# Sigmoid attention and an MLP mixer on one core: combination sums all on VectorE, the next tokens' loads queued ahead of the transposes, turns allowed anywhere in the opening section

## The chip, the cores and the metric

The kernel runs on one core of a Trainium2 chip. The metric is the device time of one execution in microseconds (us), the median of several runs. The core has five engines that work side by side, each on its own queue of instructions: TensorE (PE in the profile, with its weight loads as PEld), VectorE (DVE), ScalarE (ACT), GpSimd (POOL) and SyncE (SP). An instruction waits, at the head of its engine's queue, until everything that it needs is there, and what stands behind it waits too. DMAs are issued from such queues (here POOL for loads, SP for transposes and stores) and carried out by 16 DMA engines.

## The reference

The inputs are `q`, `k` and `v` with shape (8, 12, 448, 64) (batches, heads, tokens, features), and four weight matrices.

```python
attn = sigmoid(q @ k.T / sqrt(64) - log(448))        # 448 x 448 for each batch and head
x    = (attn @ v), heads side by side                # 8 x 448 x 768
h    = relu(x.T @ w_tok1) @ w_tok2                   # tokens mixed: 448 -> 256 -> 448
u    = x + h.T
h2   = relu(u @ w_ch1) @ w_ch2                       # channels mixed: 768 -> 1536 -> 768
out  = u + h2                                        # float32
```

## The kernel before

**Units.** The work is cut into five units. `A` and `B` are one batch each, taken as two halves of six heads; units 1, 2 and 3 are two batches each, with six pairs of heads. A unit goes through attention (for a pair: `scores` gives `qk`, ScalarE's sigmoid makes `attn` of it at L358, `values` gives `xa`), the token mixing (`tok1`, then `tok2_pair` for each of the seven rows `j` of 64 tokens, which makes `yn` on TensorE and `u = x + yn` on VectorE at L463), and two channel products, `ch1` and `ch2`. Attention and tokens of the unit behind run beside the channel products of the unit ahead; unit 3 is last and its channel products run alone.

**Channel products of units 1 to 3.** They are cut in blocks of 2 by 2 and made with seven products in place of eight. This needs combination sums of blocks. In the first product (`ch1_pieces`, 42 pieces of three matmuls: six column blocks of seven pieces) these are `s1` to `s4`, made from the transposed tokens `uT`; results are collected in PSUM banks, and three snapshots of each block, `c1`, `c6` and `c7` (`save`, L637), are copied out of a bank while it goes on being added to. VectorE then writes `h2T = relu(ps + c)` (`made`, L642) three times a block, and ScalarE a fourth one (L203). The second product (`ch2_pieces`, 25 pieces of six matmuls) has a direct product `d` of two pieces at each end, for the seventh row, and three blocks `n` of seven pieces between them. Each block needs four sums of its own, made by `row_sums` (L541) of `h2T`: `r2`, `r3`, `r4` and one in place, each 128 x 768. Block 0 has them on VectorE; blocks 1 and 2 on GpSimd in units 1 and 2, and on VectorE in unit 3. Each of the pieces of `ch2` ends in an addition to `u` on VectorE (`plus`, L849), and this addition frees the PSUM bank. There are four such banks, `m0` to `m3`: `x` of block `n` is in bank `n % 3`, `z` in bank `(n - 1) % 3`, `y` in `m3`, and the direct products in `m0` (first) and `m1` (second).

**Loads, transposes and stores.** `load_pair` loads `k`, `q` and `v` of a pair from the POOL queue (L219). Buffers of a pair are reused, and a load ahead of its time would stand in the way of other transfers, so GpSimd makes a small copy first, the *gate* (`load_next`, L338), which reads something that must be there before the loads behind it may start: the `qT` of the pair before, or, once the last pair of a unit has been scored (`state["mixing"]`), the last row of `uT` of that unit. GpSimd then brings `k` and `q` into another order (`pk`, `pq`, L279), and from the SP queue DMA transposes make `kT` and `qT` of them (L306). The seven rows of `u` are copied to half precision (`u16`, which takes a slot of the pool of `attn`) and transposed by DMA to `uT` (L478, SP queue). Finished rows of the output are stored from the SP queue too (L704), two stores to a row.

In units A and B, and for the first pair of unit 1, TensorE turns `k` and `q` itself (`turn_by_pe`, `tk` and `tq`, L291).

**What sets the order.** All engines run instructions in the order in which the program was written out. This order comes from a planner (`merge`), which keeps its own clocks for the engines: `did` adds the cost of a step to a clock, and `there` notes when a result is to be had. It takes from several lists: `main` (the pieces of the channel products), `sec` (attention and tokens of the next unit, with due positions in `main`), `side` (the sums, each with a position from which it may be written and one by which it must), `loads` (gates and transposes, as soon as their estimated time has come), `turns` and `quick`. So a change of an engine, a bank or a condition also moves other work. Ahead of `merge`, `first_attention` writes the opening section, unit A's attention, by the same estimates; a candidate there is the step that can start first:

```python
soon = when(quick[0][0]) if quick else None
...
if turns and (soon is None or soon > clock["pe"] + 1.0):
    yield turns[0][0], lambda: turns.pop(0)[1]()
```

## Time and profile before

| | |
|---|---|
| median of the runs | 406.08 us (405.96 to 406.99, 3 runs) |
| the profiled execution | 403.87 us; its span, first to last recorded instruction, 402.1 us |
| granted TensorE clock | 1.0 |
| busy: PE, DVE, ACT, POOL | 361.3, 248.7, 183.4 and 147.5 us |
| idle time of PE within the span | 40.8 us |
| data moved by DMA | 45.43 MB, mean 113 GB/s |

Busy time is the time in which an engine had a recorded instruction running. In the rows of a timeline, the first two numbers are the start and the length in us, then come the engine (`SPq` and `POOLq` are the issue of a DMA from that queue), the line, the operation, and out<-in by the names in the program, without their numbers; the number in brackets is the idle time of the engine ahead of it, and what ended it. Rows of the form "PE x L837 <- DVE u L849: 5.4, 3, 2.1" sum up waits: who waited for whom, for how many us in all, how often, and the longest. A window's row has start, end and length, then for PE, PEld, DVE, ACT, POOL and SP the busy time and in brackets the instructions, then the granted clock, the busy share of the DMA engines and GB/s. Rows that begin with a line number group equal instructions: busy us and mean ns, then idle time ahead of them.

### The profile page before, as it was taken

The numbers are of one execution on the slowest core, as the hardware profiler recorded it, in microseconds if no ns is written. First come the engines' busy times: TensorE is split into PE (matmuls) and PEld (weight loads), VectorE is DVE, ScalarE is ACT, GpSimd is POOL, SyncE is SP. The second block draws the span as 40 slices with busy tenths as digits, with TensorE's granted clock in tenths as the row PEclk, the third lists the DMA queues.
The fourth block names the chain that finished last, engine by engine and source line by source line (L and its number), as shares of the span: only waits on it lengthen the run. The fifth ranks groups of instructions, "written<-read, shape, count | busy, mean of one in ns | idle before, by whom it ended". The sixth has DMA issues, their size and how long they took to land. (4 is left out here: it accounts for less than half of the span.)

```text
span 402.1 us, 8717 instructions
## 1 busy us (share of the span) xinstructions
PE 361.3 (90%) x3600; PEld 186.1 (46%) x3600; DVE 248.7 (62%) x436; ACT 183.4 (46%) x221; POOL 147.5 (37%) x218
## 2 busy tenths in 40 slices
PE   2887999999999997899979999869987999899894
PEld 1444444455544566344435454434443545444552
DVE  1356556566754687787574457736665377887762
ACT  2883465566664210656755553636775341011000
POOL 8754314555555000554578500364561400000000
PEclk9999999999999999999999999999999999999999
DMA  7999997789977234987745956967760237400054
GB/s 101 187 203 206 166 165 117 116 135 152 143 125 117 45 78 100 181 111 99 111 78 98 160 68 133 215 104 102 108 101 2 61 87 134 132 2 0 4 154 119
DMA packets 78279, 45.43 MB, mean 113 GB/s; under 512 B 51872, under 2 KB 75424, under 8 KB 78240
## 3 DMA queue, kind: packets, MB, share of 16 engines
q0 software_dynamic: 24288, 21.93, 37.8%
q1 hardware_dynamic: 53952, 22.95, 27.1%
q8 instruction: 28, 0.46, 0.5%
q14 instruction: 11, 0.09, 0.1%
HBM read 43.84 MB, written 11.01 MB: 136 GB/s over the span
## 5 line engine op out<-in xcount | busy, mean ns | idle before, releaser
L358 ACT ACTIVATE attn<-qk 128x896 f16<-128x896 f32 x126 | 110.0, 915 | 84.0 <-PE qk L351 67.2
L622 PEld LDWEIGHTS <-w 128*128 128x128 f16 x378 | 34.8, 97 | 44.2 <-issue 15.8
L637 DVE COPY c<-x 128x448 f32<-128x448 f32 x54 | 33.5, 620 | 25.4 <-PE x L622 24.6
L351 PE MATMUL qk<-qT,kT 64*64 64x448 f16 x504 | 40.5, 362 | 7.3 <-DMA qT<-pq 5.2
L622 PE MATMUL x<-uT,w 128*128 128x448 f16 x162 | 37.6, 353 | 1.2 <-DVE c L637 0.9
L849 DVE TENSOR_TENSOR u<-u,x 128x384 f32<-128x384 f32 x36 | 19.9, 552 | 17.5 <-PE x L837 17.3
L837 PEld LDWEIGHTS <-h2T 128*128 128x128 f16 x216 | 19.9, 98 | 23.2 <-issue 11.6
L219 POOL DMA_DIRECT2D k<-in_k_dram x36 | 21.4, 602 | 24.6 <-PE tk L291 15.4
L369 PE MATMUL xa<-attn,v 64*64 64x448 f16 x504 | 27.3, 352 | 3.4 <-ACT attn L358 3.4
L351 PEld LDWEIGHTS <-kT 64*64 64x64 f16 x504 | 13.2, 104 | 29.6 <-issue 23.5
L358 ACT ACTIVATE attn_B<-qk_B 128x896 f16<-128x896 f32 x21 | 18.0, 920 | 16.4 <-PE qk_B L351 16.1
L642 DVE CUSTOM_DVE_ANT_0 h2T<-z,c 128x448 f16<-128x448 f32 x36 | 22.5, 624 | 4.2 <-PE z L622 3.4
L622 PE MATMUL z<-s,w 128*128 128x448 f16 x108 | 24.6, 353 | 0.3 <-ACT h2T L203 0.3
L279 POOL COPY pq<-q 128x896 f16<-128x896 f16 x17 | 15.9, 933 | 23.7 <-DMA q<-in_q_dram 23.7
L203 ACT ACTIVATE h2T<-x 128x448 f16<-128x448 f32 x18 | 9.8, 547 | 32.2 <-PE x L622 32.2
L463 DVE TENSOR_TENSOR u<-x_nat,yn 128x384 f32<-128x384 f16 x42 | 21.0, 548 | 4.5 <-PE yn L445 3.6
L219 POOL DMA_DIRECT2D v<-in_v_dram x36 | 22.2, 646 | 1.3 <-DMA k<-in_k_dram 1.3
L358 ACT ACTIVATE attn_A<-qk_A 128x896 f16<-128x896 f32 x21 | 17.7, 928 | 10.2 <-PE qk_A L351 10.2
L219 POOL DMA_DIRECT2D q<-in_q_dram x36 | 21.8, 624 | 1.1 <-PE tq L291 0.9
L837 PE MATMUL x<-w_s,h2T 128*128 128x384 f16 x108 | 20.9, 327 | 0.1
L369 PEld LDWEIGHTS <-v 64*64 64x64 f16 x504 | 13.6, 106 | 15.7 <-issue 8.4
L837 PEld LDWEIGHTS <-r 128*128 128x128 f16 x162 | 14.7, 98 | 12.5 <-issue 3.8
(122 smaller groups left out, 613.0 us busy)
## 6 DMA issues: line engine op xcount, KB each, us to landing
out_dram<-u SPq DMA_DIRECT2D x42, 192.0 KB, 2.9
k<-in_k_dram POOLq DMA_DIRECT2D x36, 112.0 KB, 3.0
q<-in_q_dram POOLq DMA_DIRECT2D x36, 112.0 KB, 4.4
v<-in_v_dram POOLq DMA_DIRECT2D x36, 112.0 KB, 4.5
out_dram<-u SPq DMA_DIRECT2D x28, 96.0 KB, 3.3
w<-in_moe_w_ch_dram POOLq DMA_DIRECT2D x2, 1152.0 KB, 11.8
w<-in_moe_w_ch_dram POOLq DMA_DIRECT2D x1, 2304.0 KB, 18.1
k_A<-in_k_dram POOLq DMA_DIRECT2D x6, 112.0 KB, 4.4
```

Source lines behind the costliest of these rows:

```text
L203: nc.scalar.activation(out=o, in_=x, func=RELU)
L219: nc.gpsimd.dma_start(out=t[64 * side : 64 * side + 64, :, :, :], in_=src[b, h + 2 * i : h + 2 * i + 2].rearrange("h (p j) e -> p h j e", ...
L279: nc.gpsimd.tensor_copy(out=m[:, :, :, :], in_=raws[(g, i, what)].rearrange("p h j e -> p j h e"))
L351: nc.tensor.matmul(out=ps[64 * b : 64 * b + 64, h, 0:S], lhsT=kT[(g, i)][r, j, b, :], rhs=qT[(g, i)][r, :, b, :], start=True, stop=True,)
L358: nc.scalar.activation(out=at[:, :, :], in_=ps[:, :, 0:S], func=SIGMOID, bias=att_bias, scale=att_scale)
L369: nc.tensor.matmul(out=ps[b][64 * h : 64 * h + 64, :], lhsT=vf[r, h, j, :], rhs=attn[(g, i, j)][r, h, :], start=(j == 0), stop=(j == J - 1),)
L463: nc.vector.tensor_tensor(out=u_part(g, j, half), in0=x_of(g, half)[:, j, :], in1=ps[half][:, :], op=ADD)
L622: nc.tensor.matmul(out=ps[:, :], lhsT=W(p, n, cb), rhs=A[p](n), start=(first and n == 0), skip_group_check=True, stop=(n == KD - 1),)
L637: nc.vector.tensor_copy(out=s[:, :], in_=bk[(cb, "x")][:, :])
L642: nc.vector._custom_dve(dve_ops.TENSOR_ADD_SAT, out=h[half][:, cb, :, b, :], in0=ps.rearrange("c (j p) -> c j p", j=J), in1=snap[(cb, n)]. ...
L837: nc.tensor.matmul(out=ps[:, :], lhsT=A(p, n, kb), rhs=W(p, kb), start=(first and kb == 0), skip_group_check=True, stop=(kb == KC - 1),)
L849: nc.vector.tensor_tensor(out=u, in0=u, in1=ps[:, :], op=ADD)
```

## The change

- **Sums.** The block sums of `ch2` are all made on VectorE in units 1 and 2. Block 0's are split: four of the six column blocks (`k` 0 to 4, 512 elements) may be made from piece 31 of the first product on, the rest when that is done. In unit 3 the four sums of that first part go to GpSimd, everything else to VectorE. 
- **Snapshots.** In unit 3, `c1` and `c6` are copied by ScalarE (`BY_ACT`), `c7` as before by VectorE.
- **Banks.** The first direct product uses bank `m3`, the second `m0` (`DIRECT`).
- **Stores.** In unit 3 the second store of each row is issued from ScalarE's queue.
- **Loads.** `load_next` is called two rounds earlier (`LOAD = 1`). The condition of the gate is worked out when it is written, and the `uT` comes into it only from the first row on whose transpose was written (`state["turned"]`), not from the end of scoring on: in the order that results, the gates at the two unit boundaries read `qT` of the pair before.
- **Opening section.** A turn is a candidate at any time.

```diff
@@
     DMAT, DMAU = 1.6, 1.6
     PATIENT = 6
     SLACK = 1.2
+    LOAD = 1
+    BY_ACT = (1, 6)
+    DIRECT = (3, 0)
     FROM = (10, 44)
     LATE, MIX = 8, 46
     TAKE = (5,)
@@
         if at and PAIRS.index(at) >= BY_PE:
             turn_by_dma(*at)
 
-    loads, state = [], {"mixing": None}
+    loads, state = [], {"turned": None}
 
     def load_next(g, i):
 
         at = ahead(g, i, 2)
         if not at or PAIRS.index(at) < BY_PE + 1:
             return
-        t, keys = state["mixing"], [("q", *ahead(g, i, 1))]
-        if t is not None:
-            keys.append(("uT", t, J - 1))
+        def keys():
+            t = state["turned"]
+            return [("q", *ahead(g, i, 1))] + ([("uT", t, J - 1)] if t is not None else [])
 
         def f():
             gate = pa.tile([1, 2], FP16, tag="gate", bufs=2, name=f"gate_{g}_{i}")
-            if t is None:
-                source = qT[ahead(g, i, 1)][0:1, 0, 0, 0:2]
+            last = max(keys(), key=lambda key: there[key])
+            if last[0] == "q":
+                source = qT[last[1:]][0:1, 0, 0, 0:2]
             else:
-                source = uTs[t][0:1, NDB - 1, J - 1, 0, 0:2]
+                source = uTs[last[1]][0:1, NDB - 1, J - 1, 0, 0:2]
             nc.gpsimd.tensor_copy(out=gate[:, :], in_=source)
-            did("pool", 0.2, keys, ["gate"])
+            did("pool", 0.2, keys(), ["gate"])
             load_pair(*at)
 
         loads.append((keys, f))
@@
         copy(engine_of(g), u16[:, :], u_of(g, j)[:, :])
         evac(engine_of(g), D if engine_of(g) == "act" else DH, [("u", g, j)], [("u16", g, j)])
         did("sp", 1.4, [("u16", g, j)], [("uT", g, j)], DMAU)
-        if j == J - 1:
-            state["mixing"] = None
+        state["turned"] = g
         if g not in uTs:
             uTs[g] = pa.tile([128, NDB, J, 2, P], FP16, tag="uT", bufs=1, name=f"uT_{g}")
         nc.sync.dma_start_transpose(
@@
             one(1, engine, s1, a21, a22, ADD, needs),
             one(2, engine, s2, s1, a11, SUB, needs + key(1)),
             one(4, engine, s4, a12, s2, SUB, needs + key(2)),
-            one(3, nc.vector, a21, a11, a21, SUB, needs + key(1)),
+            one(3, engine, a21, a11, a21, SUB, needs + key(1)),
         ]
 
     def ch1_sums(g, j0, j1):
@@
             if p == 1:
                 bk[(cb, "x")] = bank(f"x1_{g}_{cb}", [128, S], at=cb % 3)
                 mm(bk[(cb, "x")], 1, cb, True)
-                save(cb, 1, "dve")
+                save(cb, 1, "act" if g == 3 and 1 in BY_ACT else "dve")
...
@@
         there[("stored", g, j)] = clock["pe"] + 3.5
         did("sp", 1.3, [], [])
         for b in range(2):
-            nc.sync.dma_start(
+            (nc.scalar if g == 3 and b else nc.sync).dma_start(
                 out=out[2 * g + b].rearrange("(p j) d -> p j d", j=J)[:, j, :],
                 in_=us[(g, j)][64 * b : 64 * b + 64, :],
             )
@@
         def blk(half, j):
             return h[half][:, :, j, :, :].rearrange("c k b p -> c k (b p)")
 
-        def sums(n):
-            S2[n] = [
-                pa.tile(
-                    [128, KC, 128],
-                    FP16,
-                    tag=f"s{m}" if n == 1 else f"r{m}",
-                    bufs=1,
-                    name=f"r{m}_{g}_{n}",
-                )
-                for m in (2, 3, 4)
-            ]
+        def sums(n, k0, k1):
+
+            if n not in S2:
+                S2[n] = [
+                    pa.tile(
+                        [128, KC, 128],
+                        FP16,
+                        tag=f"s{m}" if n == 1 else f"r{m}",
+                        bufs=1,
+                        name=f"r{m}_{g}_{n}",
+                    )
+                    for m in (2, 3, 4)
+                ]
+            k = slice(k0, k1)
             return row_sums(
-                nc.gpsimd if n and g < 3 else nc.vector, KC * 128, ("R", g, n), [("h", g)], blk(0, 2 * n), blk(1, 2 * n), blk(0, 2 * n + 1), blk(1, 2 * n + 1), *[s[:, :, :] for s in S2[n]]
+                nc.gpsimd if g == 3 and n == 0 and k1 < KC else nc.vector,
+                (k1 - k0) * 128,
+                ("R", g, n) if k1 == KC else ("r", g, n, k0),
+                [("h", g)],
+                *[
+                    blk(half, j)[:, k, :]
+                    for half, j in ((0, 2 * n), (1, 2 * n), (0, 2 * n + 1), (1, 2 * n + 1))
+                ],
+                *[s[:, k, :] for s in S2[n]],
             )
 
         def A(p, n, kb):
@@
 
         def direct(half, part):
             j = 2 * NB
-            pe(0.49, [("h", g)] + ([f"m{half}"] if part == 0 else []), ["pe"])
+            pe(0.49, [("h", g)] + ([f"m{DIRECT[half]}"] if part == 0 else []), ["pe"])
             if part == 0:
-                bk[("d", half)] = bank(f"d2_{g}_{half}", [128, DH], at=half)
+                bk[("d", half)] = bank(f"d2_{g}_{half}", [128, DH], at=DIRECT[half])
             ps = bk[("d", half)]
             for cb in range(part * KC, part * KC + KC):
                 if cb % KC == KC // 2:
...
@@
                     )
             else:
                 keys = [("raw", *at, "k"), ("raw", *at, "q")]
-                loads.append((keys, lambda: turn_by_dma(*at)))
-        if j == 3:
+                loads.append((lambda: keys, lambda: turn_by_dma(*at)))
+        if j == LOAD:
             load_next(g, i)
 
     def turned_back(g, i):
@@
 
     def value_stay(g, i):
         values(g, i)
-        if i == NPAIR[g] - 1 and g not in SINGLE:
-            state["mixing"] = g
         turned_back(g, i)
 
     def attention_stays(pairs):
@@
             soon = when(quick[0][0]) if quick else None
             if quick:
                 yield quick[0][0], lambda: quick.pop(0)[1]()
-            if turns and (soon is None or soon > clock["pe"] + 1.0):
+            if turns:
                 yield turns[0][0], lambda: turns.pop(0)[1]()
             if w:
                 yield w[0][0], lambda: w.pop(0)[1]()
@@
...
             c2, b1 = base[g] + 42, base[g] + B1
-            for n, first in enumerate((c2, c2, b1)):
+            for n, k0, k1, first, span in (
+                (0, 0, 4, base[g] + 31, 11),
+                (0, 4, KC, c2, 4),
+                (1, 0, KC, c2, 7),
+                (2, 0, KC, b1, 7),
+            ):
+                name = ("R", g, n) if k1 == KC else ("r", g, n, k0)
                 for m in range(4):
-                    done = {0: [], 1: [("R1", g, n)], 2: [("R2", g, n)], 3: [("R1", g, n)]}[m]
-                    side.append((first, first + 4 if n == 0 else first + 7, [("h", g)] + done, block_sum(n, m)))
+                    keys = [("h", g)] + [[], ["1"], ["2"], ["1"]][m]
+                    keys = keys[:1] + [(name[0] + x, *name[1:]) for x in keys[1:]]
+                    side.append((first, first + span, keys, block_sum(n, k0, k1, m)))
 
         def w_sum(m):
             def f():
```

`memo` is the dictionary of the unit's pieces, which the sums now use directly. Further places only pass the new bank numbers and call the keys of `loads` as functions.

What the planner makes of it, at three places. On VectorE, where the first product of unit 2 ends and the second begins (`h2T` the result of the first, `r2` to `r4` the sums, a second `h2T` the sum in place, `d2` the first direct product, `x2` the first block), before:

```order
L642 ISA h2T_2_1_4089<-z1_2_5_4568,c6_2_5_4562 128x7x64
L541 TENSOR_TENSOR r2_2_0_4677<-h2T_2_0_4088,h2T_2_1_4089 128x768
L541 TENSOR_TENSOR r3_2_0_4678<-r2_2_0_4677,h2T_2_0_4088 128x768
L541 TENSOR_TENSOR h2T_2_0_4088<-h2T_2_0_4088 128x6x128
L541 TENSOR_TENSOR r4_2_0_4679<-h2T_2_1_4089,r3_2_0_4678 128x768
L849 TENSOR_TENSOR u_2_6_3972<-u_2_6_3972,d2_2_0_4670 128x384
L541 TENSOR_TENSOR h2T_2_0_4088<-h2T_2_0_4088 128x6x128
L849 TENSOR_TENSOR u_2_0_3828<-u_2_0_3828,x2_2_0_4750 128x384
```

and now:

```order
L645 ISA h2T_2_1_4055<-z1_2_5_4649,c6_2_5_4618 128x7x64
L544 TENSOR_TENSOR r2_2_0_4542<-h2T_2_0_4054,h2T_2_1_4055 128x256
L544 TENSOR_TENSOR r3_2_0_4543<-r2_2_0_4542,h2T_2_0_4054 128x256
L544 TENSOR_TENSOR r4_2_0_4544<-h2T_2_1_4055,r3_2_0_4543 128x256
L544 TENSOR_TENSOR h2T_2_0_4054<-h2T_2_0_4054 128x2x128
L544 TENSOR_TENSOR r2_2_1_4706<-h2T_2_0_4054,h2T_2_1_4055 128x768
L544 TENSOR_TENSOR r3_2_1_4707<-r2_2_1_4706,h2T_2_0_4054 128x768
L544 TENSOR_TENSOR r4_2_1_4708<-h2T_2_1_4055,r3_2_1_4707 128x768
L544 TENSOR_TENSOR h2T_2_0_4054<-h2T_2_0_4054 128x6x128
L863 TENSOR_TENSOR u_2_6_3960<-u_2_6_3960,d2_2_0_4695 128x384
L863 TENSOR_TENSOR u_2_0_3790<-u_2_0_3790,x2_2_0_4758 128x384
```

Two thirds of block 0's sums have moved further ahead, block 1's four sums have come from GpSimd, and the addition of `d2` stands behind all of them.

On the SP queue, where unit 1 ends and unit 2's rows are transposed (`uT_2` those rows, `u_1` the rows of unit 1 that are stored, two stores to a line here, `kT_3_2` and `qT_3_2` the transposes of the third pair of unit 3), before:

```order
L478 DMA_TRANSPOSE uT_2_3833<-u16_2_4_3935 128x6x128
L478 DMA_TRANSPOSE uT_2_3833<-u16_2_5_3954 128x6x128
L704 DMA out_0_dram<-u_1_3_2568 64x768 x2
L478 DMA_TRANSPOSE uT_2_3833<-u16_2_6_3975 128x6x128
L704 DMA out_0_dram<-u_1_4_2587 64x768 x2
L704 DMA out_0_dram<-u_1_5_2679 64x768 x2
L704 DMA out_0_dram<-u_1_6_2711 64x768 x2
L306 DMA_TRANSPOSE kT_3_2_4158<-pk_3_2_4156 128x7x128
L306 DMA_TRANSPOSE qT_3_2_4162<-pq_3_2_4160 128x7x128
```

and now:

```order
L481 DMA_TRANSPOSE uT_2_3795<-u16_2_5_3940 128x6x128
L481 DMA_TRANSPOSE uT_2_3795<-u16_2_6_3963 128x6x128
L707 DMA out_0_dram<-u_1_2_2505 64x768 x2
L707 DMA out_0_dram<-u_1_3_2578 64x768 x2
L707 DMA out_0_dram<-u_1_4_2597 64x768 x2
L707 DMA out_0_dram<-u_1_5_2689 64x768 x2
L707 DMA out_0_dram<-u_1_6_2721 64x768 x2
L309 DMA_TRANSPOSE kT_3_2_4112<-pk_3_2_4110 128x7x128
L309 DMA_TRANSPOSE qT_3_2_4116<-pq_3_2_4114 128x7x128
```

The last transposes of `uT_2` have moved ahead of the stores of rows 2 and 3, and the transposes of the pair stand behind five stored rows.

On VectorE at the end of unit 3's first product (`c1`, `c6`, `c7` the snapshots), before:

```order
L637 COPY c1_3_5_5378<-x1_3_5_5374 128x448
L642 ISA h2T_3_0_5203<-y1_3_5_5380,c1_3_5_5378 128x7x64
L637 COPY c6_3_5_5392<-x1_3_5_5374 128x448
L642 ISA h2T_3_1_5204<-z1_3_4_5364,c6_3_4_5358 128x7x64
L637 COPY c7_3_5_5405<-x1_3_5_5374 128x448
L642 ISA h2T_3_1_5204<-z1_3_5_5398,c7_3_5_5405 128x7x64
L642 ISA h2T_3_1_5204<-z1_3_5_5398,c6_3_5_5392 128x7x64
```

and now:

```order
L645 ISA h2T_3_0_5211<-y1_3_5_5388,c1_3_5_5386 128x7x64
L645 ISA h2T_3_1_5212<-z1_3_4_5372,c6_3_4_5366 128x7x64
L640 COPY c7_3_5_5413<-x1_3_5_5382 128x448
L645 ISA h2T_3_1_5212<-z1_3_5_5406,c7_3_5_5413 128x7x64
L645 ISA h2T_3_1_5212<-z1_3_5_5406,c6_3_5_5400 128x7x64
```

`c1` and `c6` are gone from this engine; they are on ScalarE, which has one copy more for each.

24 lines of the change are left out of this document (12 added, 12 removed).

## The prediction

> **What bounds the kernel now.** I read the busy shares first, then who waited for whom on TensorE (PE), then the timeline at each wait. This row of the page gives busy us per engine:
>
> ```profile
> PE 361.3 (90%) x3600; PEld 186.1 (46%) x3600; DVE 248.7 (62%) x436; ACT 183.4 (46%) x221; POOL 147.5 (37%) x218
> ```
>
> TensorE does 361.3 us of work in a span of 402.1, and the change leaves the number of its matmuls as it is. So at most 41 us are to be had, some 10 of them before the first load lands and after the last matmul. What the change can win is TensorE's waits; here are the groups that bear on it (us in total, times, longest), and one of GpSimd (POOL):
>
> ```profile
> PE x L837 <- DVE u L849: 5.4, 3, 2.1
> PE qk L351 <- DMA qT<-pq: 5.2, 5, 3.1
> PE xa L369 <- ACT attn L358: 3.4, 2, 1.8
> POOL gate L338 <- DMA uT<-u: 51.8, 2, 29.8
> ```
>
> The waits lie at the starts of the units' second channel products (L837), at the two unit boundaries where transposes and loads compete (qk, xa, gate), and, by the rows of part 3, in the last unit, which has no attention beside it to fill gaps.
>
> **1. Sums of units 1 and 2 leave GpSimd.** Second product of unit 2:
>
> ```profile
> 297.42 2.00 POOL L541 TENSOR_TENSOR r<-h2T,h2T 128x768 f16<-128x768 f16 x1 [1.13 <-DVE h2T L642]
> 297.96 1.87 DVE L541 TENSOR_TENSOR r<-r,h2T 128x768 f16<-128x768 f16 x1
> 299.76 1.99 DVE L541 TENSOR_TENSOR h2T<-h2T 128x768 f16<-128x768 f16 x1
> 303.59 0.54 DVE L849 TENSOR_TENSOR u<-u,d 128x384 f32<-128x384 f32 x1
> 304.18 1.14 PE L837 MATMUL x<-w,h2T 128*128 128x384 f16 x6 [1.95 <-DVE u L849]
> 373.04 0.55 DVE L541 TENSOR_TENSOR r<-h2T,h2T 128x768 f16<-128x768 f16 x1
> ```
>
> A VectorE sum takes 0.55 us when GpSimd is quiet (373.04) and 1.87 to 1.99 while GpSimd makes its own. The u addition that frees the bank of `d` stands behind these, and TensorE behind it. Of the 5.4 us, 1.42 is unit 3 (below), so 4.0 belong to units 1 and 2. After the change, four sums over the last third of block 0 and up to four whole ones stand ahead of that addition: at most 4 x 0.55 + 4 x 0.55 = 4.4 us, and on another bank (`m3`), so that TensorE first has `d` (two pieces of 0.97, the 1.14 of a row of six less some 0.17 in which the next piece already runs), attention, and the first `x` piece before it needs it. I take the whole 4.0; the ends are 4.0 and, if the eight sums are not covered, 2.
>
> The price: twelve sums of 0.55 us, 6.6 us, come to VectorE, and part of them falls where the next unit's tokens are made. This window of before is that stretch (us, then busy us of PE, PEld, DVE, ACT, POOL), and below it the group of the token matmuls `yn`:
>
> ```profile
> 234.30:250.50 16.20, 16.17 (x130) 8.21 (x130) 12.58 (x26) 7.33 (x9) 0.00 (x0) 1.00 0.61 99
> L445 PE MATMUL yn<-h1T,w_tok_n 128*64 128x384 f16 x168 | 17.0, 329 | 0.0
> ```
>
> In the new order VectorE has, between the first and the last `yn` of unit 2, 14 token additions, 8 u additions and 3 sums, 25 x 0.55 = 13.8 us; TensorE has 14 groups of four `yn` (17.0/168 x 4 = 0.40) and 8 main pieces of 0.97, 13.4 us. That is no spare time. I charge 1 us; ends 0 and 3.
>
> **2. The unit boundaries.** From unit 1 to unit 2:
>
> ```profile
> 251.10 1.29 SPq L478 DMA_TRANSPOSE uT<-u  x1
> 252.09 1.52 PE L369 MATMUL xa<-attn,v 64*64 64x448 f16 x28 [1.62 <-ACT attn L358]
> 252.49 3.80 SPq L704 DMA_DIRECT2D out_dram<-u  x6
> 253.97 0.27 POOL L338 COPY gate<-uT 1x2 f16<-1x2 f16 x1 [21.93 <-DMA uT<-u]
> 262.74 1.22 SPq L306 DMA_TRANSPOSE kT<-pk  x1
> 266.80 0.38 PE L351 MATMUL qk<-qT,kT 64*64 64x448 f16 x4 [3.07 <-DMA qT<-pq]
> 278.21 0.17 POOL L338 COPY gate<-qT 1x2 f16<-1x2 f16 x1 [4.23 <-DMA qT<-pq]
> 288.59 0.17 POOL L338 COPY gate<-qT 1x2 f16<-1x2 f16 x1 [2.69 <-DMA qT<-pq]
> ```
>
> The gate holds the loads of the pair 3_2 for 21.93 us until the last `uT` has landed; 12.8 us later its `qT` is there and TensorE has stood 3.07. In the new order that gate waits for the `qT` of the pair before, so k, q and v are in SBUF long before. What is late next is SP: the two transposes of 3_2 stand behind the last `uT` and five stores. Three stores took 3.80 us, so five take 6.3: about 252.4 + 6.3 = 258.7 against 262.74, 4 us earlier, more than the 3.07. The store of row 3 no longer stands ahead of the last `uT`, and the `yn` come earlier, so the 1.62 goes as well. Then the chain gate to gate sets the pace: 266.80 to 278.21 to 288.59 is 11.4 and 10.4 us, beside about 10 us of TensorE work for a pair (10.4 less some 0.5, the mean of the four shorter waits in the qT group: (5.2 - 3.1)/4). The lead of 1 us is eaten by the second or third pair. Together: 5.2 (all qT waits) + 1.6 - 1.0 = 5.8; ends 2.5 and 6.8. (The other `xa` wait, 1.8 at the first boundary, stays: its transposes keep their place.)
>
> At the first boundary a GpSimd copy of the same late pair runs into a VectorE sum:
>
> ```profile
> 166.28 2.02 DVE L541 TENSOR_TENSOR s<-uT,s 128x1344 f16<-128x1344 f16 x1
> 166.63 0.95 POOL L279 COPY pk<-k 128x896 f16<-128x896 f16 x1
> 168.89 0.73 PE L622 MATMUL y<-uT,w 128*128 128x448 f16 x3 [0.59 <-DVE x_nat L400]
> 255.71 0.84 DVE L541 TENSOR_TENSOR s<-uT,s 128x1344 f16<-128x1344 f16 x1
> ```
>
> 2.02 against 0.84: with the copy made some 25 us earlier the 1.2 goes, and with it the 0.59 and a part of the next wait: 0.9; ends 0 and 1.2.
>
> **3. Unit 3.** Its first product, from the windows and the timeline, and the two copies:
>
> ```profile
> 342.28:370.58 28.30, 25.21 (x128) 12.27 (x127) 23.25 (x39) 3.19 (x6) 0.00 (x0) 1.00 0.13 42
> 342.28 0.73 PE L622 MATMUL x<-uT,w 128*128 128x448 f16 x3
> 342.48 0.55 DVE L849 TENSOR_TENSOR u<-u,d 128x384 f32<-128x384 f32 x1 [1.23 <-PE d L889]
> 353.21 0.73 PE L622 MATMUL x<-s,w 128*128 128x448 f16 x3 [0.20 <-DVE c L637]
> 353.77 1.30 PE L622 MATMUL z<-s,w 128*128 128x448 f16 x6
> 357.54 0.73 PE L622 MATMUL x<-s,w 128*128 128x448 f16 x3 [0.20 <-DVE c L637]
> 369.35 0.73 PE L622 MATMUL x<-uT,w 128*128 128x448 f16 x3 [0.71 <-DVE c L637]
> 374.11 1.14 PE L837 MATMUL x<-w,h2T 128*128 128x384 f16 x6 [1.42 <-DVE u L849]
> L637 DVE COPY c<-x 128x448 f32<-128x448 f32 x54 | 33.5, 620 | 25.4 <-PE x L622 24.6
> L203 ACT ACTIVATE h2T<-x 128x448 f16<-128x448 f32 x18 | 9.8, 547 | 32.2 <-PE x L622 32.2
> ```
>
> A block of 21 matmuls takes 4.33 us (353.21 to 357.54); three take 0.567 without a wait (353.21 to 353.77), so 42 groups take 23.8 and 28.3 - 23.8 = 4.5 us are lost to VectorE, which is 23.25 of 28.3 us busy. Two copies of each block, 12 x 0.62 = 7.4 us, go to ScalarE, which has only the relu there; its evacuation of this size takes 0.547 and two groups (1.13 us) lie between a copy and the matmul that needs it. The last copy (369.35: 0.71, and 0.16 to start again) stays on VectorE, and I leave 0.4 for the first block: 4.5 - 0.87 - 0.4 = 3.2 won; ends 2 and 3.6.
>
> Against it stands a bank: the second `d` moves from `m1` to `m0`, the bank of the first `x` of the next unit. TensorE started that `x` at 342.28, while the u addition that now frees the bank ran from 342.48 to 343.03. So it starts 0.8 us later, and 0.35 at unit 2, where two qk groups lie between: 1.1 lost; ends 0.6 and 1.5.
>
> At the second product the wait of 1.42 goes with the first `d` on `m3` and two thirds of the sums made on GpSimd ahead of time; but the `x` of block 0 now waits for its own u addition behind two more sums. I leave 0.6 of 1.6 (1.42 and a start): 1.0 won; ends 0 and 1.6. GpSimd's four sums do not slow the product's own VectorE work if that reads PSUM: the u addition at 303.59, with GpSimd at rest, and the ones beside its sums both take 0.54 to 0.55.
>
> **4. The tail.** Stores of the last row, and one microsecond of the DMA engines (their busy share is the last but one column):
>
> ```profile
> 396.43 2.42 SPq L704 DMA_DIRECT2D out_dram<-u  x3
> 399.00:400.00 1.00, 0.00 (x0) 0.00 (x0) 0.00 (x0) 0.00 (x0) 0.00 (x0) 1.00 0.87 266
> ```
>
> SP issues the last two stores one after the other; on two queues the last one starts 0.6 us sooner. I take 0.4, since the engines are 0.87 busy behind it; ends 0 and 0.6. The Trainium skill (DMA: Bandwidth & Descriptors, Issuing engines are not separate DMA queues) speaks against it: all queues share 16 DMA engines, so a second one saves issue time alone. By that rule with the engines as the limit the term is 0 and the sum 0.4 less; the 0.87 leaves both open.
>
> **5. The opening section.** Its 20 us and the two waits of the turns:
>
> ```profile
> 20.00:40.00 20.00, 16.55 (x278) 9.29 (x275) 12.48 (x24) 12.10 (x15) 10.50 (x16) 1.00 1.20 204
> 32.15 0.58 PE L291 MATMUL tk_B<-ident,k_B 128*64 128x128 f16 x14 [0.98 <-DVE uT_A L531]
> 34.74 0.96 PE L497 MATMUL k_A<-x_nat_A,w_tok_t 64*128 64x128 f16 x28 [0.71 <-DVE qT_B L296]
> ```
>
> TensorE idles 3.45 us. The turn of pair B_0 moves ahead, into the stretch where ScalarE's sigmoids hold TensorE anyway, but in the new order the turn of B_1 takes its old place and meets the same two waits. I take 0.8; ends -0.5 and 2.
>
> **The sum**, against the profiled execution's own 403.87 us (span 402.1 and 1.8 around it): 4.0 - 1.0 + 5.8 + 0.9 + 3.2 - 1.1 + 1.0 + 0.4 + 0.8 = 14.0 us, so 389.9. The median of the runs shown is 406.08, 2.2 above that execution, and it is what a median after stands beside: 406.08 - 14.0 = 392.1. A change of 0.3%, 1.2 us, is about what measurement tells from none.
>
> **Rivals.**
> (a) The pair chain takes the place of the waits. With the gap closed, TensorE asks for a pair every 10 us while gate to gate took 10.4 and 11.4. If eight pairs of units 2 and 3 each lose 0.8, 6.4 us are given back: 398.5. For it: the 5.2 us of qT waits that are there already. Against it: two buffers each of kT and qT, and the start is 4 us earlier.
> (b) The same chain, slower than before: SP holds the transposes behind stores and GpSimd's loads meet them. The slowest interval, 253.97 to 266.80, is 12.8. If all eight pairs ran at that, 2.8 each or 22.4 us, the total would be 414. It decides at 14 / 8 = 1.75 above 10, a mean of 11.75. Against it: the 12.8 had the stores of a whole unit in it, and the others did not.
> (c) VectorE becomes the bound where tokens are made, and the waits move there: 3 us in each of two units instead of 1 in all, 397.
> (d) It does not do what it says: what the gate released early is held by SP until the old time, and only parts 1 and 3 count: 4.0 - 1.0 + 3.2 - 1.1 + 1.0 + 0.4 = 6.5, 399.6.
> (e) More goes than I count, all the upper ends of parts 1 to 5 together: 4.0 - 0 + 6.8 + 1.2 + 3.6 - 0.6 + 1.6 + 0.6 + 2.0 = 19.2, 386.9.
>
> **Chances.** Forecast 0.50 (388.5 to 395.5 is its own range), (a) 0.14, (c) 0.10, (d) 0.09, (e) 0.11, (b) 0.03, none of these but no change 0.03. From 386 to 399.5 the range leaves out (b), no change, half of (d) and a little of (e). Faster by over 0.3%: 0.93; within it: 0.03; slower: 0.04.
>
> **What the profile after would show.** Right: all VectorE sums of 768 at 0.55 us; no PE wait on u above 1 us at the second products of units 1 and 2; the two gates at the boundaries wait for qT and fall before the `uT` transposes; a block of unit 3's first product in about 3.97 us; 0.8 us ahead of unit 3's first `x`. Wrong: qk waiting for qT by over 1 us at several pairs (a, b), `yn` or `x` pieces waiting for u additions in the token stretch (c), kT of 3_2 at the same distance from the last `uT` as before (d).

## The result

The changed kernel takes 388.84 us (median of 4 runs, 386.75 to 389.14) against 406.19 (405.96 to 406.99, one run more than in the table above) for the kernel before: a ratio of 0.9559, with a 95% interval of 0.9523 to 0.9594. That is 17.3 us less, where 14.0 and a median of 392.1 were forecast. The two profiled executions, both at a granted clock of 1.0, take 403.87 and 388.77 us, 15.1 less, and their spans 402.1 and 386.9. The forecast of the profiled execution was 389.9.

The page of the changed kernel, busy time by engine:

```profile
PE 358.5 (93%) x3600; PEld 185.2 (48%) x3600; DVE 240.9 (62%) x444; ACT 189.7 (49%) x233; POOL 131.0 (34%) x210
```

TensorE's idle time in the span went from 40.8 to 28.4 us, 12.4 less; its busy time fell by 2.8 with the same 3600 matmuls. Together they are the 15.2 of the span. By the prediction's own figure a piece that follows without a gap runs 0.16 to 0.17 us into the end of the piece ahead, so each wait that is gone gives that back too: the timeline has 47 waits of TensorE of 0.2 us and more before and 30 after, and 17 x 0.16 = 2.7. Lines stand 3 to 14 further down in this kernel (L351 is L355, L622 is L625, L837 is L851, L849 is L863, L338 is L342). Its waits of TensorE (us in all, times, longest):

```profile
PE tk_A L294 <- DMA k_A<-in_k_dram: 6.4, 2, 5.3
PE y L625 <- DVE x_nat L404: 3.3, 3, 1.4
PE xa L373 <- ACT attn L362: 1.8, 1, 1.8
PE qk L355 <- DMA qT<-pq: 1.4, 2, 0.8
PE x L625 <- DVE c L640: 0.9, 2, 0.7
PE d L903 <- DVE x_nat L404: 0.4, 1, 0.4
PE x L851 <- DVE u L863: 0.3, 1, 0.3
```

Of TensorE's groups shown before, x on u went from 5.4 to 0.3, qk on qT from 5.2 to 1.4 (both waits that are left lie in units A and B, at 102 and 112 us) and xa on attn from 3.4 to 1.8. Two more rows of before belong here:

```profile
PE x L622 <- DVE c L637: 3.5, 9, 1.0
PE y L622 <- DVE x_nat L400: 0.6, 1, 0.6
```

x on c went from 3.5 to 0.9. And one group grew: `y` and `d` wait for `x_nat` four times, 3.7 us in all, where before there were the one wait of 0.6 and one of 0.3 in a second product. This is how the largest of the four looks:

```profile
173.55 0.55 PE L402 MATMUL xb<-ident,xT 128*128 128x128 f16 x7
173.57 0.61 DVE L640 COPY c<-x 128x448 f32<-128x448 f32 x1
174.22 0.62 DVE L645 CUSTOM_DVE_ANT_0 h2T<-z,c 128x448 f16<-128x448 f32 x1
174.76 0.61 DVE L640 COPY c<-x 128x448 f32<-128x448 f32 x1
175.29 0.61 DVE L404 COPY x_nat<-xb 128x896 f16<-128x896 f16 x1
175.96 0.73 PE L625 MATMUL y<-uT,w 128*128 128x448 f16 x3 [1.36 <-DVE x_nat L404]
```

`xb` turns a pair's result back, through bank `m3`; VectorE must copy it to `x_nat` before the bank is free, and three other VectorE steps stand ahead of that copy. `y` needs the same bank and is the next main piece.

Where the time went, by place. I cut each span at two points of the timeline: the first `x` of unit 1's first product, and the last matmul. The last column is what the span has left. Each row is the profiled execution of a kernel; the lower ones are explained below. The kernel with both the rule for xb and the bank ran in two forms; the profiled execution of the first (391.89 us) was in a slow state, so the second form stands here and the first form's median, below, leaves that execution out.

| kernel | median us | span | to unit 1's first x | from there to the last matmul | rest |
|---|---|---|---|---|---|
| before | 406.19 | 402.1 | 162.6 | 234.2 | 5.3 |
| changed | 388.84 | 386.9 | 161.2 | 220.2 | 5.5 |
| changed, sums back on GpSimd | 388.62 | 386.4 | 158.9 | 221.9 | 5.5 |
| changed, gates wait for uT again | 392.98 | 391.0 | 159.8 | 225.8 | 5.5 |
| changed, snapshots on VectorE | 390.74 | 389.3 | 161.4 | 222.4 | 5.5 |
| changed, second d on m1 | 387.21 | 385.3 | 159.4 | 220.4 | 5.5 |
| changed, old rule for turns | 391.05 | 389.2 | 163.6 | 220.1 | 5.5 |
| changed, rule for xb | 385.06 | 384.5 | 161.6 | 217.3 | 5.5 |
| changed, rule for xb, d on m1, one store queue | 386.53 | 384.8 | 160.7 | 218.8 | 5.4 |
| before, sums on VectorE, split | 397.97 | 397.3 | 163.4 | 228.7 | 5.3 |
| before, gates wait for qT | 401.29 | 399.9 | 163.9 | 230.1 | 5.9 |
| before, split alone | 401.95 | 401.3 | 162.9 | 233.0 | 5.4 |
| before, first d on m3 | 401.32 | 398.7 | 164.2 | 229.1 | 5.4 |

The first column of places matters for reading the rest: TensorE's order up to unit 1 is the same in the changed kernel and in those with the sums, the snapshots or `d` moved, and yet it took 161.2, 158.9, 161.4 and 159.4 us. That spread of 2.5 us, with the instructions in one and the same order, hides an effect of 1 us in a median. Edits to units 1 to 3 are therefore judged by the column behind it, edits to the opening by this one. The kernel before had medians of 407.22, 407.42 and 406.52 us when it ran beside the later kernels, beside which the changed one was not run again; so a difference of medians of 1 us from the changed kernel says little.

One more thing lies in these columns. In some of the executions the granted clock was 0.50 for a few us. This is the stretch around 260 us in the kernel whose gates wait for uT again (the clock is the last column but two), and a piece of three matmuls in it, which takes 0.73 us elsewhere:

```profile
258.00:260.00 2.00, 0.00 (x0) 0.10 (x1) 0.00 (x0) 0.00 (x0) 0.00 (x0) 0.95 0.63 141
260.00:262.00 2.00, 1.63 (x8) 0.58 (x8) 0.00 (x0) 0.92 (x1) 1.30 (x3) 0.50 0.00 0
262.00:264.00 2.00, 2.00 (x11) 0.84 (x13) 1.25 (x2) 0.06 (x1) 2.00 (x5) 0.69 0.96 124
260.89 1.30 PE L629 MATMUL x<-uT,w 128*128 128x448 f16 x3
```

The three clocks amount to about 3.4 us at 0.50, so I estimate that such a stretch costs up to 1.7 us where TensorE is busy. Ahead of the last matmul there are such stretches in the executions of the sums back on GpSimd (at 158 us), the gates (157 and 260), the old rule for turns (34), and of the last four rows of the table, in their order at 176; 162 and 302; 176 and 268; 34 and 161. The others, before and changed among them, have none.

### The profile page after: what moved, and what is told of

The parts are those of the page before. It is cut to its first block, busy times and chain, and to the rows that moved or that the text cites. A ratio compares the mean times of both kernels' runs of the same rounds, so it can differ in the third digit from the quotient of the medians.

```text
span 386.9 us, 8741 instructions
## 1 busy us (share of the span) xinstructions
PE 358.5 (93%) x3600; PEld 185.2 (48%) x3600; DVE 240.9 (62%) x444; ACT 189.7 (49%) x233; POOL 131.0 (34%) x210
## 4 chain that ended last, share of the span: by engine, by line
PE 65%; DMA 11%; DVE 8%; issue 6%; POOL 5%; ACT 3%; SPq 1%; POOLq 0%; DVEq 0%; ACTq 0%
PE x L625 11%; PE x L851 8%; DMA q<-in_q_dram 6%; PE z L625 5%; PE qk L355 5%; PE xa L373 4%; PE z L851 4%; PE k L416 4%; PE yn L449 3%; PE c_B L726 3%; PE y L625 3%; PE c_A L726 2%; PE y L851 2%; PE d L903 2%; DMA out_dram<-u 2%
## 5 line engine op out<-in xcount | busy, mean ns | idle before, releaser
L625 PEld LDWEIGHTS <-w 128*128 128x128 f16 x378 | 34.6, 98 | 45.5 <-issue 17.6
L355 PE MATMUL qk<-qT,kT 64*64 64x448 f16 x504 | 39.6, 361 | 2.7 <-DMA qT<-pq 1.4
L640 DVE COPY c<-x 128x448 f32<-128x448 f32 x42 | 26.1, 622 | 23.2 <-PE x L625 22.0
L625 PE MATMUL x<-uT,w 128*128 128x448 f16 x162 | 37.6, 353 | 1.8 <-DVE c L640 0.9
L342 POOL COPY gate<-qT 1x2 f16<-1x2 f16 x16 | 3.3, 206 | 96.7 <-DMA qT<-pq 96.7
L863 DVE TENSOR_TENSOR u<-u,x 128x384 f32<-128x384 f32 x36 | 19.9, 553 | 16.2 <-PE x L851 15.7
L851 PEld LDWEIGHTS <-h2T 128*128 128x128 f16 x216 | 19.8, 98 | 17.1 <-issue 5.3
L625 PE MATMUL z<-s,w 128*128 128x448 f16 x108 | 24.2, 353 | 0.0
L544 POOL TENSOR_TENSOR r<-h2T,h2T 128x512 f16<-128x512 f16 x1 | 1.1, 1148 | 67.4 <-DVE h2T L645 67.4
L355 PEld LDWEIGHTS <-kT 64*64 64x64 f16 x504 | 12.7, 104 | 23.6 <-issue 20.3
L194 ACT ACTIVATE u<-u 128x768 f16<-128x768 f32 x14 | 11.8, 843 | 19.1 <-DVE u L467 19.0
L851 PEld LDWEIGHTS <-r 128*128 128x128 f16 x162 | 14.9, 98 | 12.9 <-issue 4.0
```

The costliest lines, as they stand in the source:

```text
L355: nc.tensor.matmul(out=ps[64 * b : 64 * b + 64, h, 0:S], lhsT=kT[(g, i)][r, j, b, :], rhs=qT[(g, i)][r, :, b, :], start=True, stop=True,)
L625: nc.tensor.matmul(out=ps[:, :], lhsT=W(p, n, cb), rhs=A[p](n), start=(first and n == 0), skip_group_check=True, stop=(n == KD - 1),)
L640: nc.vector.tensor_copy(out=s[:, :], in_=bk[(cb, "x")][:, :])
L851: nc.tensor.matmul(out=ps[:, :], lhsT=A(p, n, kb), rhs=W(p, kb), start=(first and kb == 0), skip_group_check=True, stop=(kb == KC - 1),)
L863: nc.vector.tensor_tensor(out=u, in0=u, in1=ps[:, :], op=ADD)
```

## Experiments

**Sums back on GpSimd.** Against the changed kernel:

```diff
-nc.gpsimd if g == 3 and n == 0 and k1 < KC else nc.vector
+nc.gpsimd if (g == 3 and n == 0 and k1 < KC) or (g < 3 and n) else nc.vector
```

with the sum in place on VectorE, where it was in the kernel before too: of the four sums of blocks 1 and 2, three were on GpSimd there.

> The changed kernel, with the block sums n = 1 and 2 of units 1 and 2 back on GpSimd (three of four sums; the one in place stays on VectorE); banks and the split of block 0 stay. Theory 1 (the engine of the sums is what won part 1): the sums on VectorE take 1.9 us beside GpSimd again and the waits of 2 us at the second products of units 1 and 2 return, less the 1 us that VectorE gets back: 3.0 us slower than the changed kernel, about 391.8. Theory 2 (the bank m3 and the early two thirds of block 0 won it, the engine did not): no wait of x on u above 0.5 us, and the time within 1 us of the changed kernel's 388.8.

Measured 388.62 us (388.10 to 390.38), as the changed kernel; from unit 1 on, 1.7 us more in the trace. The collision of the sums is back, in unit 1:

```profile
204.40 1.62 DVE L547 TENSOR_TENSOR r<-r,h2T 128x256 f16<-128x256 f16 x1
205.73 1.15 PE L906 MATMUL d<-w,h2T 128*128 128x384 f16 x6
205.95 1.64 POOL L547 TENSOR_TENSOR r<-r,h2T 128x768 f16<-128x768 f16 x1
206.05 1.68 DVE L547 TENSOR_TENSOR r<-h2T,r 128x256 f16<-128x256 f16 x1
207.85 0.54 DVE L866 TENSOR_TENSOR u<-u,d 128x384 f32<-128x384 f32 x1
208.06 1.15 PE L854 MATMUL x<-w,h2T 128*128 128x384 f16 x6
```

Even so `x` starts without a wait, 0.2 us after the u addition began: it is in `m0`, and `d` in `m3`. In unit 2 it starts without one too, but there `xb`, which needs `m3`, waits for the u addition that the slow sums hold up:

```profile
292.55 0.54 DVE L866 TENSOR_TENSOR u<-u,d 128x384 f32<-128x384 f32 x1
293.14 0.55 PE L402 MATMUL xb<-ident,xT 128*128 128x128 f16 x7 [1.15 <-DVE u L866]
```

Of theory 1 the slow sums came true, and one wait in another place; theory 2 is right about the waits of x on u and about the time. So the engine of the sums is worth at most 1.7 us where the bank and the split are there, and part of that can be the stretch at half clock at the start of unit 1.

**The same part done alone.** The kernel before, with the split and the sums of units 1 and 2 on VectorE, banks (0, 1):

```diff
-nc.gpsimd if n and g < 3 else nc.vector
+nc.vector
-(0, 0, KC, c2, 4)
+(0, 0, 4, base[g] + 31, 11), (0, 4, KC, c2, 4)     # units 1 and 2
```

> The kernel before with one part of the change: the block sums of units 1 and 2 on VectorE, block 0's in two parts; the banks of the direct products, unit 3, loads and opening as before. Theory 1 (the engine of the sums): the two waits of x on u (2.07 and 1.95 us) fall below 0.5 us each, 3 to 4 us faster than before, about 402.7. Theory 2 (the bank): eight sums stand ahead of the u addition that frees the first x's bank, and about 1.5 us of each wait stay: less than 1.5 us faster, above 404.7.

Measured 397.97 us (397.22 to 399.46) against 407.22 for the kernel before beside it, ratio 0.9773 (0.9700 to 0.9847): 9 us, over twice what theory 1 gave. The spans differ by 4.8, with one stretch at half clock in the later one. The waits of x on u in units 1 and 2 are 0.6 us in all, as theory 1 said. The rest is in the main a side effect that neither theory had: with GpSimd's sums gone from its clocks, the planner writes the `yn` earlier (the last ones end 5.8 us ahead of the second `d` in place of 2.9), and the 1.62 us of xa at the boundary of units 1 and 2 goes as well.

**The split alone and the bank alone.** The kernel before with the second edit of the last diff only, and, in another, with nothing but

```diff
-DIRECT = (0, 1)
+DIRECT = (3, 1)
```

> The kernel before with the split alone: block 0's sums of units 1 and 2 in two parts (both on VectorE, as before), blocks 1 and 2 on GpSimd, banks as before. Theory 1 (each of split, engine and bank cures the waits of x on u by itself): the 2.07 and 1.95 us fall below 0.7 each. Theory 2 (the engine is needed where the bank is the old one, since three sums of the last third still take 1.2 us each beside GpSimd): at least 1 us of each wait stays. By the trace 1 to 4 us less than before.

Measured 401.95 us (400.74 to 403.04), ratio 0.9884 (0.9835 to 0.9933). TensorE's order is the same as before, instruction by instruction. In unit 1 the wait stays, in unit 2 it is gone:

```profile
210.97 0.65 PE L855 MATMUL x<-w,h2T 128*128 128x384 f16 x3 [1.95 <-DVE u L867]
```

Theory 1 fails in unit 1, theory 2 in unit 2. From unit 1 on it saves 1.2 us, with two stretches at half clock in it, which can hide up to 3.4 us more; the medians differ by 4.6.

> The kernel before with one bank changed: the first direct product on m3, the second on m1 as before, the sums as before on two engines and unsplit. Theory 1 (the first x waits only because d shares its bank): the two waits of x on u in units 1 and 2 vanish, but y, which uses m3, waits for the same u addition, one piece later, 1 us of each wait. Theory 2 (the queue of VectorE holds the next u addition as well): the waits stay as long and move to y. By the trace 0 to 3 us less than before, unit 3's own wait of 1.42 under 0.5.

Measured 401.32 us (400.45 to 402.84), ratio 0.9873 (0.9824 to 0.9922), and 5.1 us less from unit 1 on. What is left at the two second products moved to the third piece of a block. It adds to the bank of the block's first piece and so has to wait for the u addition that reads it, which stands behind slow sums on VectorE:

```profile
222.09 0.65 PE L855 MATMUL x<-w_s,r 128*128 128x384 f16 x3 [0.39 <-DVE u L867]
300.91 0.54 DVE L867 TENSOR_TENSOR u<-u,x 128x384 f32<-128x384 f32 x1
301.51 0.65 PE L855 MATMUL x<-w_s,r 128*128 128x384 f16 x3 [0.96 <-DVE u L867]
```

With one more of 0.2 these are 1.6 us. Theory 1 is right in kind (the wait is due to the shared bank; 4.0 became 1.6), wrong in units 1 and 2 in that `y` would take it over. Unit 3's 1.42 became 0.45, as it said, and there it is `y` that waits. These waits are 3.4 of the 5.1 us; the rest comes from other work that moved with the bank (qk's waits on qT fell from 5.2 to 2.0 us, unit 3's first product rose from 28.3 to 30.0). So several cures of one wait stand in the change, and each undone or done alone shows something else than its share.

**Gates wait for uT again.** The changed kernel with `state["mixing"]` and the gate's old condition, `LOAD = 3`:

> The changed kernel, with the gates at the two boundaries waiting for the last uT again, as before. Theory 1 (by the prediction's terms, 5.8 and 0.9 at the boundaries): 6.7 us slower than the changed kernel, about 395.5, with the wait of some 3 us on qT and of some 1.6 us on attn at the boundary of units 1 and 2 back. Theory 2 (the trace of the changed kernel shows four new waits, of y and d on x_nat, 3.65 us in all, and they come from the order that the early loads give): these go in this kernel, and it is 6.7 - 3.6 = 3.1 us slower, about 391.9.

Measured 392.98 us (391.67 to 395.20): 4.1 us slower, in the medians as in the spans; 5.6 from unit 1 on. The waits of `y` and `d` on `x_nat` are gone here, as theory 2 says, and the two at the boundary are back:

```profile
245.21 1.52 PE L376 MATMUL xa<-attn,v 64*64 64x448 f16 x28 [0.88 <-ACT attn L365]
260.37 0.59 PE L358 MATMUL qk<-qT,kT 64*64 64x448 f16 x4 [3.92 <-DMA qT<-pq]
```

The size lies between the theories, nearer to the second, and the two stretches at half clock (157 and 260 us), of which the changed kernel's execution has none, can account for up to 2.3 of the 5.6: what is left is near theory 2's 3.1. (Of the two edits to the loads, the earlier position alone does nothing: with `LOAD = 3` and the new gate the order of all five engines is that of the changed kernel.)

**The same part alone.** The kernel before with the new gate:

> The kernel before with one part of the change: the gates at the two boundaries wait for qT of the pair before. Theory 1 (the prediction's terms stand by themselves): 6.7 us faster, about 399.5. Theory 2 (new waits of y on x_nat, 3.3 us, take half of it back): about 3.4 us faster, 402.8. A third possibility, that the loads which now come early meet GpSimd's sums of 2 us each, which stand in the same queue ahead of the gates: less than 2 us faster.

Measured 401.29 us (400.48 to 402.18), ratio 0.9851 (0.9778 to 0.9924): 5.9 us less than the kernel before beside it, 4.1 less from unit 1 on, 2.2 less in the span. The mechanism is theory 2's: `y` waits for `x_nat` 3.8 us in all. The size is not decided: 3.4 and 6.7 were expected, the two measures lie between, and the trace has two stretches at half clock. Beside that the wait of x on u is gone in unit 1 and has grown in unit 2, where in the new order VectorE has one sum more ahead of the u addition:

```profile
298.26 1.98 DVE L541 TENSOR_TENSOR r<-h2T,r 128x768 f16<-128x768 f16 x1
300.17 0.54 DVE L541 TENSOR_TENSOR h2T<-h2T 128x768 f16<-128x768 f16 x1
300.64 0.54 DVE L849 TENSOR_TENSOR u<-u,d 128x384 f32<-128x384 f32 x1
301.24 1.00 PE L837 MATMUL x<-w,h2T 128*128 128x384 f16 x4 [2.74 <-DVE u L849]
```

So the early loads alone pay 2.74 there where 1.95 stood before, and in the whole change that wait is gone: the parts done alone do not simply add up.

**Snapshots of unit 3 on VectorE** (`BY_ACT = ()`):

> The changed kernel, with all snapshots of unit 3 on VectorE again (banks, GpSimd's part of the sums and the stores stay). Theory 1 (VectorE bounded that product): a block of unit 3's first product takes 4.33 us again, and the time is 2.9 us longer (the stage from the first x to the first d was 28.30 us before and is 25.37), about 391.7. Theory 2 (part of it came from the sums that left VectorE's queue there): below 1.5 us.

Measured 390.74 us (389.41 to 393.10), 1.9 slower, and 2.2 from unit 1 on. A block takes 4.33 us again (341.29 to 345.62):

```profile
336.95 0.73 PE L625 MATMUL x<-s,w 128*128 128x448 f16 x3 [0.27 <-DVE c L640]
341.29 0.73 PE L625 MATMUL x<-s,w 128*128 128x448 f16 x3 [0.20 <-DVE c L640]
345.62 0.73 PE L625 MATMUL x<-s,w 128*128 128x448 f16 x3 [0.20 <-DVE c L640]
```

The stage is 27.75 us, 2.4 above the changed kernel's 25.37: theory 1, but 0.5 of its 2.9 is not the snapshots'.

**Second direct product on m1** (`DIRECT = (3, 1)`):

> The changed kernel, with the second direct product on bank m1, as before, and the first on m3. Theory 1 (the shared bank m0 holds the first x of the next unit until the u addition is done): TensorE starts unit 3's first x 1.95 us after the second d in place of 2.76, and unit 2's some 0.3 earlier: 1.1 us faster, about 387.7. Theory 2: VectorE, which makes the combination sums at that place, holds the second group instead, and nothing is gained: within 0.4 us.

Measured 387.21 us (386.79 to 390.71), 1.6 less. But the table puts all of it ahead of unit 1, where nothing is changed; from unit 1 on it is 220.4 against 220.2. The first `x` of units 2 and 3 does start 0.8 us sooner (1.95 us behind the second `d`, not 2.76), and the stage behind unit 2's is 1.7 longer (42.8 against 41.1). Theory 1 is right about the bank, theory 2 about the sum.

**The old rule for turns** in the opening section:

> The changed kernel, with the old rule for turns in the opening section. Theory 1 (the trace: unit 1's first product begins 1.36 us earlier after the change, of which the first load gave 0.27 and a second load took 0.8 back): 1 to 2 us slower, about 390.3. Theory 2 (the difference of the two openings is that of their loads): within 0.5 us.

Measured 391.05 us (390.29 to 393.80), 2.2 slower, all of it ahead of unit 1 (163.6 against 161.2). All executions of the table with the old rule reach unit 1 between 162.6 and 164.2 us, all with the new one between 158.9 and 161.6, and within each group TensorE's order up to there is one and the same. The means are 163.4 and 160.4: 3 us, of which I estimate up to 0.7 to be stretches at half clock, more of which lie in the first group. That is well above theory 2.

**A rule for xb.** The changed kernel, with a condition on the two places where the planner takes from `quick`:

```diff
+def clear():
+    n = nxt[0]          # the main piece that is written next
+    return not ("m3" in quick[0][0] and n < len(main) and "m3" in main[n][2])
...
-if quick and t_of(quick[0][0]) <= now:
+if quick and clear() and t_of(quick[0][0]) <= now:
```

> The changed kernel with one more rule in the planner: a transpose back (xb, which needs bank m3) is not written where the next piece of the main product needs m3 too (y, or the first d). Theory 1 (the new waits of y and d on x_nat are a collision on that bank alone): the 3.65 us go, about 385.2. Theory 2 (VectorE is late there anyway, and TensorE waits for another of its copies): less than 1.5 us faster, above 387.3.

Measured 385.06 us (384.22 to 387.20), ratio to before 0.9446 (0.9402 to 0.9490), 3.8 less than the changed kernel. Its waits of TensorE have no `y` or `d` on `x_nat`; the wait ahead of unit 3's first `x`, 0.65 in the changed kernel, is 1.2 now, and from unit 1 on the gain is 2.9:

```profile
PE xa L373 <- ACT attn L362: 1.8, 1, 1.8
PE c_B L766 <- DVE u L776: 1.3, 2, 0.9
PE x L625 <- DMA uT<-u: 1.2, 1, 1.2
```

Theory 1 holds for the waits, and some of what they gave turns up again later. This version is the fastest of all.

**Both, and the queue of the last stores.** The same rule with `DIRECT = (3, 1)`, once with the changed kernel's stores and once with all stores on SyncE:

> The changed kernel with the rule that keeps a transpose back away from the pieces that need its bank, and the second direct product on m1: both gains add up, 3.8 and 1.6 us, about 383.5. The rival: what one frees the other waits for (the first x of unit 3 waited 1.2 us with the rule alone), and it is within 1 us of the 385.1 of the rule alone.

> The same kernel with unit 3's stores all on SyncE's queue. Theory 1 (the second queue saves issue time at the end): 0.4 us slower than with ScalarE's queue; from the last matmul to the end of the span 5.9 us against 5.5. Theory 2 (the DMA engines bound the tail): the same within 0.2 us.

The first took 387.2 us (385.92 to 388.06), the second 386.53 (385.10 to 389.05). The gains do not add up, and the rival is right in kind: what one frees the other waits for. In the second kernel unit 3's first product is 26.2 us in place of 25.4, for its `x` waits for sums that VectorE has not made yet. But both medians are above the 386.1 that the rival allowed; why the bank costs 1.5 to 2.2 us on top of the rule is not shown beyond that. The second store queue saves nothing: without it the median is 0.7 lower, within the spread of the runs. Behind the last matmul lie 5.5 us in each of the kernels with two store queues, 5.3 to 5.9 in those with one. The window of that stretch, of before and then of the changed kernel, ends with the DMA engines' busy share and their GB/s:

```profile
396.77:402.10 5.33, 0.18 (x2) 0.00 (x0) 0.55 (x1) 0.00 (x0) 0.00 (x0) 0.97 0.60 180
```

```profile
381.43:386.90 5.47, 0.18 (x2) 0.00 (x0) 0.56 (x1) 0.00 (x0) 0.00 (x0) 1.00 0.57 181
```

The rule of the Trainium skill that was weighed in the prediction (DMA: Bandwidth & Descriptors, Issuing engines are not separate DMA queues) is that a second queue saves issue time alone. The runs agree: even that issue time, 0.6 us on paper, did not come out at the end.

## Why the prediction was right, point by point

The steps, as the prediction sized them, and what the traces gave:

| term | forecast us | measured us | from |
|---|---|---|---|
| 1 waits of x on u | 4.0 | 4.0 | none above 0.2 left in units 1 and 2 |
| 1 VectorE's price | -1.0 | 0 | window of 206 to 247 us, below |
| 2 boundary, qT and xa | 6.8 less 1.0 | 6.8 | no qT wait behind unit B, one xa wait less |
| 2 (not forecast) y and d on x_nat | 0 | -3.7 | the group that grew |
| 2 first boundary | 0.9 | 1.0 | the waits of 0.59 and 0.43 are gone |
| 3 first product of unit 3 | 3.2 | 2.9 | 28.30 to 25.37 |
| 3 bank m0 | -1.1 | -0.8 | unit 3: 1.95 to 2.76; unit 2's is won back behind it |
| 3 second product of unit 3 | 1.0 | 0.9 | 24.26 to 23.35 |
| 4 tail | 0.4 | -0.1 | 5.33 to 5.47 |
| 5 opening | 0.8 | 1.4 | 162.6 to 161.2; about 3 by the means |
| rest, not forecast | 0 | 2.8 | what is left to 15.2 |

The rest is restarts and short waits. Between the first `x` of unit 1 and that of unit 3, TensorE's busy time fell by 1.3 us, and its idle time by 8.8, of which the terms above hold 7.3; the 1.5 beyond them are in the main waits of under 0.5 us that the prediction did not count. (Of the whole fall of 2.8 in busy time, 0.8 lie in the opening and 0.8 in unit 3's first product, 25.21 to 24.40, and are in those terms already.)

That the total came out within 1.2 us is in part luck. What came out better than forecast adds up to 5.8 us, what came out worse to 4.6, and the largest part of each, the rest and the new waits on `x_nat`, was not forecast at all.

**Right in place and size:** the waits of x on u (with too narrow a reason, below), unit 3 and its bank. Unit 3's blocks, from one x on `s` to the next, came out at the forecast 3.97 us:

```profile
335.89 0.73 PE L625 MATMUL x<-s,w 128*128 128x448 f16 x3
339.86 0.73 PE L625 MATMUL x<-s,w 128*128 128x448 f16 x3
343.83 0.73 PE L625 MATMUL x<-s,w 128*128 128x448 f16 x3
```

So did the SP queue at the boundary: five rows of stores took 6.32 us, 6.3 were forecast, and `kT` of the pair goes out behind them, 6.5 us after the last `uT` where it was 10.4 before, with no wait of TensorE on it later:

```profile
234.92 6.76 SPq L481 DMA_TRANSPOSE uT<-u  x4
241.78 6.32 SPq L707 DMA_DIRECT2D out_dram<-u  x10
248.21 1.60 SPq L309 DMA_TRANSPOSE kT<-pk  x1
```

**Too narrow a reason in part 1.** The step "sums leave GpSimd" was given the whole 4.0 us. By the experiments, the sums on VectorE with the split take away 3.4 of the waits' 4.0 by themselves, the split alone 2.1, the bank alone 2.4, and in the changed kernel no x waits with the sums on GpSimd either (1.15 us come back as a wait of `xb`). The prediction named the split and the bank, but as asides; it did not see that each does much of the work without the others. (The sums on VectorE without the split were not run.)

**Missed in part 2.** "What is late next is SP" named the wrong place. The pairs came early enough, and two of the lists that feed TensorE now met on a bank: `xb` ahead of `y`, 3.7 us. (That VectorE has more sums to make is not the reason: with the sums back on GpSimd the waits of `y` are 3.3 us as well, and with the old gate they are gone.) The words of the prediction that fit it best, "`yn` or `x` pieces waiting for u additions", look for it in the token stretch, not there. This loss was offset by two terms that were too small: the chain of gates cost nothing, where 1.0 was charged, and the end of the pipe that each wait costs was counted in unit 3 only.

**Rivals.** (a) and (b) did not come: no qk waits for qT behind unit B. Of (a) the slow pace is there, the gates of unit 2's pairs are 10.1 to 11.6 us apart, but TensorE does not ask for the pairs any faster; the last gates are 10.0 and 10.2 apart.

```profile
254.40 0.18 POOL L342 COPY gate<-qT 1x2 f16<-1x2 f16 x1 [24.06 <-DMA qT<-pq]
264.43 0.17 POOL L342 COPY gate<-qT 1x2 f16<-1x2 f16 x1 [2.70 <-DMA qT<-pq]
274.64 0.17 POOL L342 COPY gate<-qT 1x2 f16<-1x2 f16 x1 [2.68 <-DMA qT<-pq]
```

(The gate at 254.40 still waits long, for `qT` of the first pair behind the boundary.) (c) did not come: in the stretch of unit 2's tokens TensorE is idle for 0.13 of 41 us, in that of unit 3's for 0.4 of 40.

```profile
206.00:247.00 41.00, 40.87 (x341) 20.48 (x339) 26.25 (x56) 18.99 (x24) 11.44 (x18) 1.00 0.74 133
```

(d) did not come either, as `kT` at 248.21 shows. (e), more than was counted, is half true: by the profiled executions 15.1 us is nearer to the 14.0 of the forecast than to the 19.2 of (e), but the median of 388.84 is nearer to its 386.9 than to 392.1.

**The tail and the opening.** The tail's 0.4 was taken although the row quoted there showed the DMA engines 0.87 busy, and that row was right. The opening was given 0.8 of the 3.45 us that TensorE idled there, since the second turn "meets the same two waits". It met one of them, the 0.71; the other, 0.98 of `tk_B`, is gone. The two profiled executions differ by 1.4 us there, within the term's upper end of 2.0; by the means of all executions it is about 2.3 to 3, above it.

**Median and profile.** 15.1 us of the 17.3 are in the two profiled executions. The other 2.2 are the distance of the profiled execution of before from the median of its runs (the prediction carried it over unchanged, since it adds the saving to the median); the last section says what is known of it.

## What to carry to other kernels

When a wait ends with a bank becoming free, list everything that would free it sooner (another bank, the work ahead of the last reader, the engine that slows it) and expect any one of them to do: undoing one part then shows nothing and tells nothing about its worth. When one stream is moved earlier, look at which bank its next step shares with the main stream, and at what stands ahead of the reader of that bank on its engine; a short rule in the planner won more here (3.8 us in the median, 2.9 from unit 1 on) than a second store queue did. Cut each execution at a point behind the loads before comparing small edits: here the same order took 158.9 to 161.6 us to reach unit 1. And look at the granted clock along the span, not at its mean alone.

## What the runs showed of the hardware that was not expected

A VectorE sum beside a GpSimd sum took about as long as its neighbour, at a third of its size as at the whole: 128 x 256 took 1.62 and 1.68 us beside GpSimd's 1.67 and 1.64 (in the kernel with the sums back on GpSimd), where alone, in unit 3 of the changed kernel, it takes 0.29. So a third of such a sum costs nearly as much there as the whole one (1.87 to 1.99). The Trainium skill (SBUF — State Buffer, Who interferes with whom) says that a VectorE instruction with two inputs in SBUF contends with a GpSimd instruction that reads SBUF, for a pair of ports that they share under an exclusive lock; these numbers agree. The u additions with one input in PSUM took 0.54 in the same place.

The granted clock was 1.00 or, for about 3.4 us at a time, 0.50. Outside the last us of a span, each of the stretches at half clock that are named under the table began within 1 us of the end of a wait of TensorE of 0.7 to 3.9 us (3.92 at 260 us, in the rows there). Such a wait is not enough: the profiled execution of before has waits of 1.78, 2.07 and 3.07 us and no such stretch. A mean clock a little below 1 counts these stretches: 0.989 in the kernel with the gates, with two of them ahead of the last matmul and a third behind it.

The kernel before ran at a mean of 0.975 to 0.996 in all of the runs beside the other kernels, from 404.21 us at 0.992 to 411.04 at 0.976, and at 1.0 in its own profiled execution; the changed kernel ran at 0.995 to 1.0. This fits that medians fell by more than the spans of executions near 1.0, as in the kernel with the sums alone (9 us in the medians, 4.8 in the spans): a long wait that is gone can take a stretch at half clock with it. That the kernel before has more such stretches where its mean is 0.975 was not seen in a trace, and which of the edits keeps the clock up was not tried: both stay open.
